# Squared norms of keys and queries added by matmul, accumulators of the first expert layer given back, other ranks in the plan

## The chip, the cores and the metric

The kernel runs on one core of a Trainium2 chip. The metric is device time in microseconds (us). A time is one execution; the kernel before ran three times and its median is the time before. The profile is of one further execution.

## The reference

Three layers in a row, all in float32 (weights come as 64-bit floats):

```python
def phi(x):                                  # x: [4, 8, 576, 64], omega: [128, 64]
    proj = np.einsum('bhsd,md->bhsm', x, omega)
    sq = np.sum(x * x, axis=-1, keepdims=True) / 2.0
    h = proj - sq
    h = h - np.max(h, axis=-1, keepdims=True)
    return np.exp(h) / np.sqrt(m)
q_p, k_p = (phi(q_s), phi(k_s))              # q, k scaled by 64 ** -0.25
kv = np.einsum('bhsm,bhsd->bhmd', k_p, v)
z = np.sum(k_p, axis=2)
num = np.einsum('bhsm,bhmd->bhsd', q_p, kv)
den = np.einsum('bhsm,bhm->bhs', q_p, z)[..., None] + 1e-06
x = (num / den)                              # as [2304, 512]
# first expert layer, d_ff 1536
g = x @ w_gate
x = g * (1.0 / (1.0 + np.exp(-g))) * (x @ w_val) @ w_out
# second, d_ff 2048: a piecewise quadratic of x @ w_in, then @ w_out
```

## The kernel before

**Attention.** Tokens lie on the 128 partitions for the values and on the free axis for keys and queries: one tile `ki`, `kl` or `qi` holds two layouts side by side, layout 0 with the 64 features of two heads on the partitions (`xb[:, 0]`) and layout 1 with tokens on the partitions (`xb[:, 1]`). `load` brings each with a DMA of its own. A group is one `k_group` (4 batches, 5 groups each of one or two units) or one `q_group` (9 blocks of 256 tokens, 2 halves `d`). `front` does the feature map of a group: `squares` turns layout 1 into squared norms, either with accumulating activations on ScalarE (L597) or with one square on ScalarE (L600) and one reduction on VectorE (L601); `proj` multiplies layout 0 by `omr` into two PSUM banks (L625; two 64-row halves of the array, one per head); VectorE takes the row maximum (L631) and adds the squared norm to it with two small reductions (L635); the exponential is taken by ScalarE straight from PSUM with that bias (L643), or by VectorE adding the bias (L647) and ScalarE taking the exponential in place (L651). Keys go on to the key-value sums (L690) and their copy (`kv_evac`), queries are transposed by a matmul (L763), copied into `qt`, and multiplied with the sums (`num`, L817); `norm` divides, and `x1_split` splits the block into a high and a low part in `x1s`.

**First expert layer.** `moe1` runs the early columns block by block as soon as `x1s` of a block is there: 24 matmuls of three-way split products per bank (`split3`, L400 to L402), then `elem1`, `row_out` into `hl`, and `out1`, which adds into two accumulator banks. These two banks are taken once, at the first block, and kept (`acc`); `acc_free` tells when `evac1` has read one. The rest of the first layer, and the second, run afterwards (`late_up`, `late_down`) with block products of a Strassen kind.

**What sets the order.** Nothing is scheduled by hand: `Planner` simulates the engines with given costs, takes the ready operation with the smallest rank on each engine, and emits instructions in that order, so every engine has one fixed queue. The ranks and start delays are the constants `PR_*` and `T_*`. All DMAs are issued from one queue (SP). There are 8 PSUM banks in one ring (`bank`); `bank_pair` takes two of them for a group of `front` or `num`.

Of the kernel before, what the change touches and what calls it, by code (L numbers as in the profile page):

```python
# [28 lines left out]
P = 128  # L29
# [17 lines left out]
NWL, NB1 = 7, 8  # L47
KINS, VINS, QINS, EBK, EBQ, N_QT = 3, 5, 2, 6, 4, 3
N_KL, N_QL, N_EL = 2, 1, 2

# [10 lines left out]

PR_K, PR_K0, PR_Q0, PR_Q = 1.04, 0.32, 0.17, 0.83
PR_C0, PR_C, PR_CS = 0.66, 0.90, 0.90
PR_W = 1.06
PR_BANK = 0.3
PR_ST, PR_X, PR_E = 1.50, 0.74, 1.45
T_V, T_Q0, T_C0 = 3.84, 2.87, 5.50
N_GATE, N_CS = 1, 3
N_WS = 2
# [205 lines left out]
def performer_moe_kernel(ctx: ExitStack, tc: tile.TileContext, qX, kX, vX, om, ident,  # L275
# [65 lines left out]
    omr = att.tile([P, P], F32, name="omr")  # L341
    ebufs = {False: ring(att, "ebk", EBK, [P, 512]), True: ring(att, "ebq", EBQ, [P, 512])}
    kin = ring(att, "ki", KINS, [P, 2, 512])
# [24 lines left out]
    lend(qin, "ql", N_QL, [P, 2, 512])  # L368
    lend(ebufs[False], "el", N_EL, [P, 512])
    nc.gpsimd.memset(rect.free[0][0][:, :, 32:33], 1e-6)  # L370
# [109 lines left out]
    def conv_feed():  # L480
        early = [(s, f) for p in range(NE) for s in ("g", "v", "o") for f in (2 * p, 2 * p + 1)]
        for i, kk in enumerate(early):
            if i == 0:
                yield T_C0
            if i == N_CS:
                yield q0_front
            yield from conv(kk, w_src(kk), wring, PR_C0 if i < 3 else late_rank)
        for kk in early[-2:]:
            yield wready[kk]
        for key in [kk for m, a, order, sets in passes for c in sets for kk in set_keys(m, c)]:  # L490
            t = yield Get(wtmp)
            pl.spawn(stage(key, t), PR_ST)
# [115 lines left out]

    def front(xb, n, loads, is_q, res, rng):

        st = yield Get(stat)
        sv = st.rearrange("p (a u) c -> p a u c", a=2)
        units = slice(0, 2 * n)
        sq_end = pl.spawn(squares(xb[:, 1], n, sv[:, :, :, 1], loads[1]), pl.cur.prio)
        es = []
        for a in range(2):
            es.append((yield Get(ebufs[is_q])))
        yield omr_ready
        yield loads[0]
        banks = yield from bank_pair()  # L620

        def proj():
            for u in range(2 * n):
                for a, h in enumerate(halves):
                    nc.tensor.matmul(banks[a][:, u * P:(u + 1) * P], xb[h, 0, u * P:(u + 1) * P], omr[h], start=True, stop=True,  # L625
                                     skip_group_check=True)
        yield Op("PE", 0.446 * n + 0.1, proj)
        pl.spawn(release(sq_end, rng, xb))
        pv = [ps[:, 0:256 * n].rearrange("p (u m) -> p u m", m=P) for ps in banks]
        for a in range(2):  # L630
            yield Op("DVE", c_dve(256 * n), lambda: nc.vector.tensor_reduce(  # L631
                out=sv[:, a, units, 0], in_=pv[a], axis=AX.X, op=ALU.max, negate=True))
        yield sq_end
        for i in range(2):
            yield Op("DVE", 0.12, lambda: nc.vector.tensor_reduce(  # L635
                out=sv[:, :, units, 2 + i], in_=sv[:, :, units, i:2 + i], axis=AX.X, op=ALU.add, negate=True))

        def expo(a):
            e, ps = es[a], banks[a]
            if pl.pick(ACT=2 * n * 0.262, DVE=c_dve(256 * n)) == "ACT":  # L640
# [14 lines left out]
        pl.put(stat, st)  # L655
        res.extend(es)

    kv_bank = {}

    def load(xb, src, n):  # L660
        src = src.rearrange("(p k c) -> p k c", p=P, k=2)
        return [pl.spawn(dma(xb[:, l, 0:256 * n], src[:, l], P * 1024 * n), pl.cur.prio) for l in range(2)]

    def k_group(b, gs, kb, prev):
        n = len(gs)
        es = []
        loads = load(kb, kX[b, gs[0] * 65536:(gs[0] + n) * 65536], n)
        yield from front(kb, n, loads, False, es, kin)
        for g in gs:
# [16 lines left out]
        def mm():  # L686
            for kp, v, u, pr, li in todo:
                for a in range(2):
                    for m, h in enumerate(halves):
                        nc.tensor.matmul(kp[h, 2 * pr + a, 0:65], es[a][:, u * P + 64 * m:u * P + 64 * m + 64],  # L690
                                         v[:, 65 * a:65 * a + 65], start=(li == 0 and a == 0),
                                         stop=(li == 8 or (li == 4 and pr == 0)), skip_group_check=True)
        yield Op("PE", 0.232 * len(todo) + 0.15, mm)
        for u in range(2 * n):
            i = 2 * gs[0] + u
            if i % 9 == 8:
                pl.spawn(kv_evac(b, i // 9), pl.cur.prio - 0.1)
        for e in es:
            back(ebufs[False], e)
        for g in gs:  # L700
# [32 lines left out]
    def k_stream():  # L733
        prev = Ev()
        pl.set(prev)
        for b in range(4):
# [4 lines left out]
            for gs in GROUPS:  # L741
                kb = yield Get(kin)
                prev = pl.spawn(k_group(b, gs, kb, prev), PR_K0 if b == 0 else PR_K)

    def q_group(k, d, qb):
        es = []
        yield from front(qb, 2, load(qb, qX[k, d], 2), True, es, qin)
        if k == 0:
# [7 lines left out]
        def turn(r):  # L756
            tp = yield Get(bank)

            def trans():
                for a in range(2):  # L760
                    for t in range(2):
                        u = 2 * r + t
                        nc.tensor.transpose(tp[:, (a * 2 + t) * P:(a * 2 + t + 1) * P], es[a][:, u * P:(u + 1) * P], ids)  # L763
            yield Op("PE", 4 * 0.11, trans)
            left[0] -= 1
            if left[0] == 0:
                for e in es:
                    back(ebufs[True], e)
            yield from copy(q_t[:, r].rearrange("p a t -> p (a t)"), tp, 512, False)
# [27 lines left out]
    def num(k, d, q_t):  # L797
# [11 lines left out]
        rc = yield Get(rec)  # L809
        banks = yield from bank_pair()  # L810

        def mm():
# [8 lines left out]
        yield from norm(*banks, rc, x)  # L821
        pl.put(rec, rc)
        yield from x1_split(k, d, x)
        yield from dma(half_block(x1d, k, d), x.rearrange("p (n t) -> p n t", n=2), P * 512 * 4)
# [107 lines left out]

    def evac1(k, d, last):
        rng = (osb, xin)[d] if k == NBLK - 1 else (xin, xpart)[d]
        if (k, d) in held:
            yield held_ready[k, d]
            x = held[k, d]
            yield Op("DVE", c_dve(512), lambda: nc.vector.scalar_tensor_tensor(
                out=x, in0=acc[d], scalar=0.5, in1=x, op0=ALU.mult, op1=ALU.add))
        else:  # L940
            if not last:
                held[k, d] = None
            x = yield Get(rng)
            yield from copy(x, acc[d], 512, False, 0.5)
        pl.set(acc_free[d])
        if not last:
# [63 lines left out]
    def out1(step, h_ev, res):  # L1010
# [7 lines left out]
        for n in range(KD):  # L1018
            d, c = divmod(n, 2)
            if first and c == 0:  # L1020
                yield acc_free[d]
                acc_free[d] = Ev()
            for i in range(2):
                yield Op("PE", 3 * c_pe(TB), lambda: split3(
                    acc[d][:, c * TB:(c + 1) * TB], ws[i][:, 0, n * P:(n + 1) * P], ws[i][:, 1, n * P:(n + 1) * P],
                    hl[:, 0, i * TB:(i + 1) * TB], hl[:, 1, i * TB:(i + 1) * TB],
                    first and c == 0 and i == 0, last and i == 1, True))
            if last and c == 1:
                pl.spawn(evac1(k, d, end))
        pl.put(hrow, res[1])  # L1030
# [4 lines left out]
    def moe1():  # L1035
        pend = None
        for step in steps1:
            k, fp = step
            if fp == 0:
                yield x1_ready[k]  # L1040
                if k == 0:
                    pl.set(moe_on)
                    for _ in range(2):
                        acc.append((yield Get(bank, -2)))
            xs = x1_tile[k]
# [601 lines left out]
```

## Time and profile before

| what | value |
|---|---|
| three runs | 955.35, 949.29, 953.86 us; median 953.86 us |
| the profiled execution, its own time | 949.58 us |
| its span, first to last instruction | 947.8 us |
| mean granted TensorE clock | 0.995 of full speed |
| PE (TensorE matmul) busy | 920.2 us, 97% |
| PEld (its weight loads) busy | 892.9 us, 94% |
| DVE (VectorE) busy | 799.7 us, 84% |
| ACT (ScalarE) busy | 515.2 us, 54% |
| POOL (GpSimd) busy | 67.6 us, 7% |

Busy shares are of the whole span. Matmuls are pipelined, so that a busy PE need not be a PE at its peak, and a stage is read by its own stretch of time. Of each matmul of attention with float32 operands by `omr` the trace has two records.

### The profile page before, as it was taken

Reading aid. Unit: us, or ns where it says so; the run is one execution under the profiler, and the core shown is the slowest. Engines: PE = TensorE matmul, PEld = TensorE weight load, DVE = VectorE, ACT = ScalarE, POOL = GpSimd, SP = SyncE. Lnnn points to the kernel's source line nnn. Section 1 sums busy time; section 2 is a strip of 40 time slices with the busy share of each in tenths; the row PEclk is TensorE's granted clock in tenths of the full one; section 3 lists DMA queues with packets and bytes.
Section 4 is the critical chain, followed back from the end, with each engine's and each line's share of the span. In section 5 each row is a group of like instructions: output and inputs, shape, how many; then the busy total and the mean of one; then the engine's idle time right before and its main releaser. Section 6 shows DMA issues by size and latency. Waiting matters only on the chain.

```text
span 947.8 us, 21783 instructions
## 1 busy us (share of the span) xinstructions
PE 920.2 (97%) x8708; PEld 892.9 (94%) x8708; DVE 799.7 (84%) x1536; ACT 515.2 (54%) x1226; POOL 67.6 (7%) x58
## 2 busy tenths in 40 slices
PE   7698989999999999999999999999999999999998
PEld 5588878999999999999999999999999999999998
DVE  7999998877989999999998999996698669866553
ACT  7988778653445454554454565554455445544331
POOL 0343332122100000000000000000000000000000
PEclk9899999999999999999999999999999999999999
DMA  8767596445848267665647654431323041403022
GB/s 284 272 204 238 176 292 217 168 168 184 260 166 278 64 228 226 222 209 177 190 170 232 209 181 155 137 127 63 123 68 112 6 141 46 133 13 100 1 90 90
DMA packets 91255, 152.12 MB, mean 160 GB/s; under 512 B 8592, under 2 KB 44432, under 8 KB 91152
## 3 DMA queue, kind: packets, MB, share of 16 engines
q1 hardware_dynamic: 91152, 150.72, 48.9%
q8 instruction: 68, 1.11, 0.5%
q14 instruction: 35, 0.29, 0.1%
HBM read 107.69 MB, written 42.99 MB: 159 GB/s over the span
## 4 chain that ended last, share of the span: by engine, by line
PE 64%; DVE 11%; DMA 6%; ACT 2%; issue 2%; SPq 0%; DVEq 0%; ACTq 0%
PE bank L400 20%; PE bank L401 20%; PE bank L402 20%; DMA ws<-in_w_dram 2%; DMA ws<-in_wo_dram 2%; PE bank L817 2%; DVE x1s L393 1%; PE bank L625 1%; DVE w L393 1%; DVE wt L424 1%; DVE wt L422 1%; DVE hb L1211 1%; PE bank L763 1%; DVE wb L393 1%; DVE xi L393 1%
## 5 line engine op out<-in xcount | busy, mean ns | idle before, releaser
L400 PE MATMUL bank<-x1s,w 128*128 128x256 f32 x492 | 138.7, 282 | 6.4 <-DVE hb L910 2.0
L402 PE MATMUL bank<-x1s,w 128*128 128x256 f32 x492 | 136.4, 277 | 0.0
L401 PE MATMUL bank<-x1s,w 128*128 128x256 f32 x492 | 136.3, 277 | 0.0
L400 PEld LDWEIGHTS bank<-x1s,w 128*128 128x128 f32 x492 | 92.4, 188 | 9.6 <-DVE hb L910 2.4
L402 PEld LDWEIGHTS bank<-x1s,w 128*128 128x128 f32 x492 | 92.6, 188 | 0.0
L401 PEld LDWEIGHTS bank<-x1s,w 128*128 128x128 f32 x492 | 92.4, 188 | 0.0
L400 PE MATMUL bank<-x1s,wb 128*128 128x256 f32 x286 | 79.1, 277 | 1.2 <-ACT eb L381 1.2
L402 PE MATMUL bank<-x1s,wb 128*128 128x256 f32 x286 | 79.0, 276 | 0.0
L401 PE MATMUL bank<-x1s,wb 128*128 128x256 f32 x286 | 79.0, 276 | 0.0
L400 PE MATMUL bank<-x1s,wx 128*128 128x256 f32 x278 | 77.4, 278 | 0.8 <-ACT eb L381 0.8
L381 ACT ACTIVATE x1s<-xq 128x512 fp32r<-128x512 f32 x80 | 50.2, 630 | 50.4 <-PE bank L402 20.7
L402 PE MATMUL bank<-x1s,wx 128*128 128x256 f32 x278 | 76.9, 277 | 0.6 <-POOL wx L391 0.6
L401 PE MATMUL bank<-x1s,wx 128*128 128x256 f32 x278 | 76.8, 276 | 0.0
L393 DVE TENSOR_TENSOR x1s<-xq,x1s 128x512 fp32r<-128x512 f32 x90 | 61.8, 686 | 9.6 <-ACT x1s L381 9.0
L417 ACT ACTIVATE wt<-ws 128x512 f32<-128x512 f32 x68 | 46.2, 682 | 41.7 <-DMA ws<-in_wo_dram 30.4
L381 ACT ACTIVATE eb<-bank 128x512 f32<-128x512 f32 x94 | 55.5, 591 | 22.3 <-PE bank L402 21.8
L400 PEld LDWEIGHTS bank<-x1s,wb 128*128 128x128 f32 x286 | 53.7, 188 | 1.4 <-ACT eb L381 1.4
L381 ACT ACTIVATE hlr<-hb 128x512 fp32r<-128x512 f32 x53 | 33.3, 631 | 38.8 <-PE bank L401 25.3
L402 PEld LDWEIGHTS bank<-x1s,wb 128*128 128x128 f32 x286 | 53.7, 188 | 0.0
L401 PEld LDWEIGHTS bank<-x1s,wb 128*128 128x128 f32 x286 | 53.7, 188 | 0.0
L400 PEld LDWEIGHTS bank<-x1s,wx 128*128 128x128 f32 x278 | 52.2, 188 | 1.4 <-ACT eb L381 1.2
L402 PEld LDWEIGHTS bank<-x1s,wx 128*128 128x128 f32 x278 | 52.2, 188 | 0.8 <-POOL wx L391 0.8
(247 smaller groups left out, 3347.8 us busy)
## 6 DMA issues: line engine op xcount, KB each, us to landing
ws<-in_w_dram SPq DMA_DIRECT2D x40, 512.0 KB, 4.9
ws<-in_wo_dram SPq DMA_DIRECT2D x28, 512.0 KB, 4.5
qi<-in_qX_dram SPq DMA_DIRECT2D x36, 256.0 KB, 4.7
xq<-x1d SPq DMA_DIRECT2D x36, 256.0 KB, 4.3
xq<-x2d SPq DMA_DIRECT2D x36, 256.0 KB, 3.9
ki<-in_kX_dram SPq DMA_DIRECT2D x28, 256.0 KB, 5.3
x1d<-os SPq DMA_DIRECT2D x18, 256.0 KB, 3.7
op<-os SPq DMA_DIRECT2D x18, 256.0 KB, 2.1
```

The source lines that it names most:

```text
L381: yield Op("ACT", c_act(n), lambda: nc.scalar.activation(dst, src, AF.Copy, scale=1.0 if scale is None else scale))
L393: yield Op("DVE", c_dve(n), lambda: nc.vector.tensor_tensor(out=dst, in0=a, in1=b, op=op), True)
L400: nc.tensor.matmul(ps, l_hi, r_hi, start=first, stop=False, skip_group_check=shared)
L401: nc.tensor.matmul(ps, l_hi, r_lo, start=False, stop=False, skip_group_check=shared)
L402: nc.tensor.matmul(ps, l_lo, r_hi, start=False, stop=last, skip_group_check=shared)
L417: yield Op("ACT", 0.575, lambda: nc.scalar.activation(t, hw.bitcast(F32), AF.Abs))
L422: yield Op("DVE", c_dve(512), lambda: nc.vector.scalar_tensor_tensor(out=ti, in0=lw, scalar=29, in1=ti, op0=ALU.logical_shift_right, op1=A ...
L424: yield Op("DVE", c_dve(512), lambda: nc.vector.scalar_tensor_tensor(out=ti, in0=hw, scalar=0xC0000000, in1=ti, op0=ALU.bitwise_and, op1=A ...
L625: nc.tensor.matmul(banks[a][:, u * P:(u + 1) * P], xb[h, 0, u * P:(u + 1) * P], omr[h], start=True, stop=True, skip_group_check=True)
L763: nc.tensor.transpose(tp[:, (a * 2 + t) * P:(a * 2 + t + 1) * P], es[a][:, u * P:(u + 1) * P], ids)
L817: nc.tensor.matmul(banks[what][h, r * TB + c0:r * TB + c1], kvr[b, d][:, r, a, halves[what]], q_t[:, r, a, c0:c1], start=True, stop=True, ...
L1211: yield Op("DVE", c_dve(n), lambda: nc.vector.scalar_tensor_tensor(out=h, in0=h, scalar=1.0, in1=g, op0=ALU.add, op1=ALU.mult), lock)
```

## The change

Three things. **Norms by TensorE:** for the keys of batches 0 and 1 and the queries of blocks 0 to 3, only layout 0 is loaded. Its square, times 1/16, is made into the other half of the same tile (`square_t`, on ScalarE or VectorE), and a second run of `proj` with a tile of -1 (`neg`) adds minus the squared norm onto the projection in PSUM. The row maximum then is the bias itself, and the two small reductions go. **Accumulators given back:** `out1` gets a bank when it begins a sum, and `evac1` returns it. **Ranks:** in `front` and `num` all that reads a bank pair ranks at most `PR_FRONT` = 0.35; `PR_K` is one number per batch, and other constants change. The exponential buffers of a group's two heads are now one tile.

```diff
-KINS, VINS, QINS, EBK, EBQ, N_QT = 3, 5, 2, 6, 4, 3
-N_KL, N_QL, N_EL = 2, 1, 2
+KINS, VINS, QINS, EBK, EBQ, N_QT = 3, 5, 2, 3, 2, 3
+N_KL, N_QL, N_EL = 2, 1, 1
-PR_K, PR_K0, PR_Q0, PR_Q = 1.04, 0.32, 0.17, 0.83
-PR_C0, PR_C, PR_CS = 0.66, 0.90, 0.90
+PR_K, PR_Q0, PR_Q = (0.32, 0.77, 0.91, 1.17), 0.17, 0.68
+PR_C0, PR_C, PR_CS = 0.66, 1.02, 1.13
+PR_FRONT = 0.35
-T_V, T_Q0, T_C0 = 3.84, 2.87, 5.50
-N_GATE, N_CS = 1, 3
+T_V, T_Q0, T_C0 = 3.0, 3.5, 7.0
+N_GATE, N_CS = 1, 6
+    neg = att.tile([P, P], F32, name="neg")
+    nc.gpsimd.memset(neg, -1.0)
+    def square_t(x, x2, m):
+        if pl.pick(ACT=c_act(m), DVE=c_dve(m)) == "ACT":
+            yield Op("ACT", c_act(m), lambda: nc.scalar.activation(x2, x, AF.Square, scale=0.25))
+        else:
+            yield Op("DVE", c_dve(m), lambda: nc.vector.scalar_tensor_tensor(
+                out=x2, in0=x, scalar=0.0625, in1=x, op0=ALU.mult, op1=ALU.mult), True)
...
-        sq_end = pl.spawn(squares(xb[:, 1], n, sv[:, :, :, 1], loads[1]), pl.cur.prio)
+        by_pe = len(loads) == 1
+        if not by_pe:
+            sq_end = pl.spawn(squares(xb[:, 1], n, sv[:, :, :, 1], loads[1]), pl.cur.prio)
         yield omr_ready
         yield loads[0]
+        if by_pe:
+            sq_end = pl.spawn(square_t(xb[:, 0, 0:256 * n], xb[:, 1, 0:256 * n], 256 * n), pl.cur.prio)
         banks = yield from bank_pair()
+        rank = pl.cur.rank
+        pl.cur.rank = min(pl.cur.prio, PR_FRONT)
...
-        yield Op("PE", 0.446 * n + 0.1, proj)
+        yield Op("PE", 0.446 * n + 0.1, lambda: proj(0, omr, True, not by_pe))
+        if by_pe:
+            yield sq_end
+            yield Op("PE", 0.446 * n + 0.1, lambda: proj(1, neg, False, True))
...
-                out=sv[:, a, units, 0], in_=pv[a], axis=AX.X, op=ALU.max, negate=True))
-        yield sq_end
-        for i in range(2):
-            yield Op("DVE", 0.12, lambda: nc.vector.tensor_reduce(
-                out=sv[:, :, units, 2 + i], in_=sv[:, :, units, i:2 + i], axis=AX.X, op=ALU.add, negate=True))
+                out=sv[:, a, units, 3 if by_pe else 0], in_=pv[a], axis=AX.X, op=ALU.max, negate=True))
+        if not by_pe:
+            yield sq_end
+            for i in range(2):
+                yield Op("DVE", 0.12, lambda: nc.vector.tensor_reduce(
+                    out=sv[:, :, units, 2 + i], in_=sv[:, :, units, i:2 + i], axis=AX.X, op=ALU.add, negate=True))
...
-        loads = load(kb, kX[b, gs[0] * 65536:(gs[0] + n) * 65536], n)
-        yield from front(kb, n, loads, False, es, kin)
+        loads = load(kb, kX[b, gs[0] * 65536:(gs[0] + n) * 65536], n, b > 1)
+        es = yield from front(kb, n, loads, False, kin)
...
-        yield from front(qb, 2, load(qb, qX[k, d], 2), True, es, qin)
+        es = yield from front(qb, 2, load(qb, qX[k, d], 2, k > 3), True, qin)
...
         banks = yield from bank_pair()
+        pl.cur.rank = min(pl.cur.prio, PR_FRONT)
...
             if first and c == 0:
-                yield acc_free[d]
-                acc_free[d] = Ev()
+                acc1[d] = yield Get(bank, -2)
...
-            yield from copy(x, acc[d], 512, False, 0.5)
-        pl.set(acc_free[d])
+            yield from copy(x, ps, 512, False, 0.5)
+        pl.put(bank, ps)
...
                 if k == 0:
                     pl.set(moe_on)
-                    for _ in range(2):
-                        acc.append((yield Get(bank, -2)))
```

Where the new order differs, at the two places that the prediction speaks of. The first is TensorE's queue just ahead of the first matmul of the first expert layer (that is the row with `x1s`). `omr` rows are projections, `vi` rows key-value sums, `qt` rows the numerators, `ids` rows transposes. Before:

```order
L625 MATMUL bank_70<-omr,qi_158 128x128
L625 MATMUL bank_69<-omr,qi_158 128x128
L817 MATMUL bank_66<-qt_142,kvr_0_160 64x256 x2
L817 MATMUL bank_65<-qt_142,kvr_0_160 64x256 x2
L690 MATMUL bank_64<-vi_136,ebk_145 64x65 x2
L690 MATMUL bank_64<-vi_136,ebk_146 64x65 x2
L400 MATMUL bank_70<-x1s_72,w_110 128x256
```

With the change (L639 is the projection's line, `neg` rows the added matmuls, L403 the old L400):

```order
L779 MATMUL bank_63<-ids,ebq_151 128x128 x4
L639 MATMUL bank_66<-omr,ki_154 128x128
L639 MATMUL bank_67<-omr,qi_155 128x128
L639 MATMUL bank_66<-neg,ki_154 128x128
L639 MATMUL bank_68<-omr,qi_156 128x128
L639 MATMUL bank_67<-neg,qi_155 128x128
L639 MATMUL bank_68<-neg,qi_156 128x128
L708 MATMUL bank_64<-vi_136,ebk_147 64x65 x12
L403 MATMUL bank_66<-x1s_72,w_110 128x256
```

The `x1s` row moved back: ahead of it stand now 208 projections and norm matmuls (104 with `omr`, 104 with `neg`) where there were 96, the same 108 key-value matmuls and 32 transposes, and 16 numerators in place of 32. Between a projection and its `neg` matmuls mostly another group's matmuls stand. In all the queue has 8042 matmuls instead of 7906, the 136 more being the `neg` ones.

The second place is ScalarE's queue ahead of the activation that writes the last piece of the first `x1s` block. `ebk`, `ebq` rows are exponentials, L597 accumulating squares, L600 whole squares, L417 a step of a weight's conversion. Before:

```order
L600 ACTIVATE qi_159<-qi_159 128x512
L600 ACTIVATE ki_157<-ki_157 128x512
L417 ACTIVATE wt_79<-ws_77 128x512
L643 ACTIVATE ebk_149<-bank_66,st_129 128x128 x2
L597 ACTIVATE ki_156,st_126<-ki_156 128x64 x8
L381 ACTIVATE qt_142<-bank_66 128x512
L793 ACTIVATE os_103<-bank_64 128x512
L381 ACTIVATE x1s_72<-os_103 128x512
```

With the change (L614 the square of layout 0, L661 the exponential from PSUM, L669 that in place, L384 a copy):

```order
L614 ACTIVATE ki_154<-ki_154 128x512
L384 ACTIVATE kvr_1_158<-bank_69 128x4x64
L808 ACTIVATE os_102<-bank_65 128x512
L661 ACTIVATE ebq_150<-bank_70,st_130 128x128 x4
L661 ACTIVATE ebk_149<-bank_67,st_129 128x128 x2
L661 ACTIVATE ebq_151<-bank_66,st_122 128x128 x4
L384 ACTIVATE qt_142<-bank_67 128x512
L384 ACTIVATE x1s_72<-os_103 128x512
```

What stands ahead of that row over the whole queue: before 48 L597, 9 L600, 26 L643 and 12 L651; now no accumulating square, 12 L614, 56 L661 and 6 L669; and five smaller instructions fewer. From TensorE's instruction 1757 of before on (1893 of the change) its queue is the same, 6149 matmuls long.

## Rows read from the trace of the kernel before

**Rows 1.** Page, busy time of each engine over the span

```profile
PE 920.2 (97%) x8708; PEld 892.9 (94%) x8708; DVE 799.7 (84%) x1536; ACT 515.2 (54%) x1226; POOL 67.6 (7%) x58
```

**Rows 2.** Windows: length, busy us (records) of PE, PEld, DVE, ACT, POOL; clock, DMA, GB/s

```profile
5.16:12.75 7.59, 3.41 (x41) 3.03 (x40) 5.63 (x16) 4.26 (x23) 0.00 (x0) 1.00 0.98 346
12.75:30.00 17.25, 17.25 (x294) 15.15 (x296) 17.15 (x40) 17.04 (x68) 0.11 (x1) 0.90 0.95 315
30.00:53.00 23.00, 15.72 (x176) 11.72 (x172) 22.03 (x55) 21.90 (x86) 10.63 (x8) 0.85 0.73 245
53.00:184.00 131.00, 124.92 (x1534) 112.44 (x1535) 120.34 (x262) 102.55 (x372) 40.35 (x32) 1.00 0.68 218
184.00:260.00 76.00, 76.00 (x706) 72.17 (x705) 60.88 (x116) 32.62 (x63) 16.12 (x12) 1.00 0.61 200
700.00:750.00 50.00, 50.00 (x443) 50.00 (x443) 42.76 (x77) 25.06 (x45) 0.00 (x0) 1.00 0.19 63
```

**Rows 3.** Waits of PE, 5 to 53 us: who waited for whom, total, times, longest

```profile
PE bank L625 <- DMA qi<-in_qX_dram: 3.6, 1, 3.6
PE bank L625 <- ACT ebq L643: 2.9, 1, 2.9
PE bank L625 <- ACT kvr L381: 2.0, 1, 2.0
PE bank L763 <- ACT qt L381: 1.4, 1, 1.4
```

**Rows 4.** Timeline of PE: start, us, instructions merged

```profile
53.04 0.38 PE L400 MATMUL bank<-x1s,w 128*128 128x256 f32 x1
59.67 0.39 PE L400 MATMUL bank<-x1s,w 128*128 128x256 f32 x1 [0.35 <-DVE qt L383]
...
61.24 1.16 PE L625 MATMUL bank<-omr,ki 64*128 64x128 f32 x16
62.33 0.38 PE L400 MATMUL bank<-x1s,w 128*128 128x256 f32 x1
...
67.35 1.03 PE L763 MATMUL bank<-ids,ebq 128*128 128x128 f32 x8
68.14 0.36 PE L400 MATMUL bank<-x1s,w 128*128 128x256 f32 x1
...
74.94 1.39 PE L690 MATMUL bank<-vi,ebk 128*64 128x65 f32 x40
76.25 1.16 PE L625 MATMUL bank<-omr,qi 64*128 64x128 f32 x16
...
214.56 3.67 PE L817 MATMUL bank<-qt,kvr 128*64 128x256 f32 x32
218.17 1.09 PE L763 MATMUL bank<-ids,ebq 128*128 128x128 f32 x8
```

**Rows 5.** Groups by form, 0 to 230 us: busy, mean ns, idle before

```profile
L635 DVE TENSOR_REDUCE st<-st 128x8 f32<-128x16 f32 x68 | 10.6, 162 | 0.5
L647 DVE TENSOR_TENSOR ebk<-bank,st 128x512 f32<-128x512 f32 x16 | 10.7, 684 | 0.1
```

**Rows 6.** Timeline of ACT: start, us, instructions merged

```profile
25.58 0.24 ACT L597 ACTIVATE qi<-qi 128x64 f32<-128x64 f32 x1
25.82 0.24 ACT L597 ACTIVATE qi<-qi 128x64 f32<-128x64 f32 x1
...
36.25 3.19 ACT L643 ACTIVATE ebq<-bank,st 128x128 f32<-128x128 f32 x12
39.26 0.71 ACT L651 ACTIVATE ebq<-ebq 128x512 f32<-128x512 f32 x1
39.78 0.71 ACT L600 ACTIVATE qi<-qi 128x512 f32<-128x512 f32 x1
...
47.80 0.74 ACT L381 ACTIVATE x1s<-os 128x512 fp32r<-128x512 f32 x1
```

**Rows 7.** Waits of PE, 53 to 184 us, the longest of nine

```profile
PE bank L400 <- ACT qt L381: 1.7, 1, 1.7
```

## What the change is expected to do

> **What bounds the kernel now.** I read the busy line first, then the windows by stage, then the waits of TensorE, and last its timeline for the price of each kind of matmul. TensorE is busy 97% of the span [rows 1], and from 184 to 260 us it never idles: 76.00 of 76.00 us, with VectorE at 80% [rows 2]. From its instruction 1757 on its queue is word for word the same in both kernels. So the end moves by what happens before that point, one for one: by matmul time added, less TensorE time that was lost there and no longer is. No later work can give anything back or take anything away, unless another engine falls behind.
>
> Lost time before 184 us lies in two stretches. In the head, from the first projection at 5.16 us to the first matmul on `x1s` at 53.04 us, ScalarE and VectorE bound: from 12.75 to 53 us they are busy 38.9 and 39.2 of 40.25 us, while TensorE idles 7.3 us between 30 and 53 us and its granted clock is 0.90 and 0.85, a mix of the 2.4 and 1.2 GHz levels [rows 2]. It idles 4.2 us before 12.75 us too, when the DMA share is 0.98 [rows 2]; its longest wait in the head, 3.6 us, is for a query load, the next three, 6.3 us in sum, are for ScalarE [rows 3]. In the middle, 53 to 184 us, TensorE is busy 124.9 of 131 us and VectorE 120.3 [rows 2]: the two are nearly level.
>
> **Prices.** Eight projections in a run take 62.33 - 61.24 = 1.09 us, 0.136 each; eight transposes 0.79, 0.099 each; twenty key-value matmuls 76.25 - 74.94 = 1.31, 0.066 each; sixteen wide numerators 218.17 - 214.56 = 3.61, 0.226 each [rows 4]. A matmul of the expert layers costs 50 / 443 = 0.113 [rows 2]. Twelve of them between attention runs take 61.24 - 59.67 = 1.57 us instead of 1.36 [rows 4], so each such interruption costs 0.21.
>
> **What is added.** The 136 norm matmuls have the shape and type of projections: 136 x 0.136 = 18.5 us, all on TensorE and all before 184 us. If each run cost its record's 1.16 us [rows 4], it would be 17 x 1.16 = 19.7; I take 18.5, since runs follow each other at that pace.
>
> **What the head gives back.** The order puts 96 projections, 108 key-value matmuls, 32 transposes and 32 wide numerators ahead of the first `x1s` matmul: 13.1 + 7.1 + 3.2 + 7.2 = 30.6 us of work in 47.9 us, 17.3 us lost. With the change it is 208 projections and norms, 108, 32 and 16 numerators: 28.3 + 7.1 + 3.2 + 3.6 = 42.2 us. How much of it is waited for? ScalarE's queue up to the last piece of `x1s`: 48 accumulating squares at 0.24 go (11.5), 30 exponentials from PSUM at 3.01 / 12 = 0.25 come (7.5), six exponentials in place at 0.52 go (3.1), 3 squares come, two of them half width (about 1.1), five smaller ones go (about 2) [rows 6]. That is 8 us less, where its end before was at 48 us [rows 6], so `x1s` could be there at about 40 us; 42.2 us of TensorE work from 5.16 us on ends at 47.4 us at best. TensorE becomes the head's bound. VectorE loses over the whole attention 36 small reductions at 0.16, and of full-width passes at 0.68 nine reductions of squares and nine bias additions, and gets two squares: 16.7 us less by durations [rows 5]. 18 loads, 4.5 MB, go from SP's queue, 13 us at 346 GB/s [rows 2]; the queries come no later for it, and their wait is filled with 20 norm matmuls of keys (2.7 us), 4.2 us becoming 1.5. For the rest I take 2.5 us, 7% of the 36 us left, a little more than the 3% that ScalarE and VectorE lost when they were the bound. Head loss 4.0, so **13.3 us come back** and the first `x1s` matmul starts at 51.4 us. Bounds: 2.6 (the 3% instead) and 11.8 (the three ScalarE waits of 6.3 us stay, and 4 us for load and half clock).
>
> **What the middle gives back.** Before: 131 - 124.9 = 6.1 us idle, and 39 interruptions of expert-layer work x 0.21 = 8.2; 14.3 lost. The new order has 25 interruptions, 5.3 us. Of the idle time I keep 2.7, since VectorE has less to do per matmul there. Loss 8.0, **6.3 come back**; bounds 14 (nothing, if new waits fill the room) and 5.3.
>
> How much room that stretch has can be judged in two ways. Its busy TensorE leaves 6.1 us, its weight loads 131 - 112.4 = 18.6 [rows 2]. The Trainium skill (Perfetto Trace Analysis, Identifying the Most-Contended Engine) says that matmul busy time is a poor measure of TensorE's headroom and the weight loads' busy share a good one. By the first my middle can hardly gain more than it does, by the second it could gain twice that; I take the first and keep the second as a rival.
>
> **At nothing.** The returned accumulators: none of TensorE's nine waits in the middle, the longest 1.7 us [rows 7], is for the copy of an accumulator, so nothing of the two freed banks is counted beyond the idle time taken off above; if that cover fails, these short waits are what comes back. The merged exponential buffers hold as much as before. The fill of `neg` on POOL comes ahead of its first work.
>
> **Sum.** 18.5 - 13.3 - 6.3 = -1.1 us. The profiled execution took 949.58 us (span 947.8), 4.3 below the median of the runs, 953.86; I put the difference on the median: **952.8 us**, no change that shows. About 1% of this kernel, 9.5 us, is what a measurement can tell.
>
> **Rivals.** *Slower: TensorE waits for the square.* Each norm run stands in TensorE's fixed queue and needs a square from ScalarE, queued there among exponentials; whatever stands behind it on TensorE waits too, and through it ScalarE's next exponentials. Its price is one full-width ScalarE step with its handover, 0.71 us by its record [rows 6], up to 2.9 where ScalarE is late [rows 3]. With 17 runs x 0.71 = 12.1 us, of which 2 us are in the sum's losses already, it gives 953 + 10 = 963 us. It decides (slower by 1%) from some 0.7 us a run. Against it: in the order other groups' matmuls stand between most projections and their norms. For it: ScalarE stays the producer of all that TensorE waits for in the head, and a bank pair is held longer. The Trainium skill (TensorEngine Tiling, PSUM Bottleneck) says that packing small matmuls speeds TensorE but not the emptying of PSUM, which speaks against gaining from matmuls here; the three waits for ScalarE agree with it.
>
> *Faster: all lost time but the unavoidable goes.* Head loss 2.6, middle 5.3 and no idle: 18.5 - 14.7 - 9.0 = -5.2; should the 25 interruptions cost half as much too, -7.8: 946 us. For it: the weight loads' share above, and TensorE denser in the head, so that its granted clock may stay at 2.4 GHz. Against it: VectorE still at some nine tenths in the middle.
>
> *The relief is not used.* ScalarE and VectorE are freed, but the head stays bound by order, with the first `x1s` matmul at 56 us (head loss 8.6), and the middle gains its fewer interruptions alone, 2.9: 18.5 - 8.7 - 2.9 = +6.9, 961 us.
>
> **Chances.** Forecast 0.55, its own range 948 to 958. Faster rival 0.20. Relief not used 0.12. Slower rival 0.13. The range reaches from 944 to 963 us. Faster by over 1%, below 944.3: 0.14, the far part of the faster rival and the spread of the runs. Slower by over 1%, above 963.4: 0.13, the slower rival in full, or relief not used and more. Within: 0.73.
>
> **What would show it.** Right: the first `x1s` matmul between 50 and 54 us, with a clock near full in 12 to 53 us; ScalarE and VectorE clearly under 97% there; 25 interruptions, and some 3 us of idle TensorE from there to the steady part; the same rows later, shifted by about -1 us. Wrong: waits of the `neg` rows for ScalarE of 0.5 us and more, run after run (slower), or `x1s` before 49 us (faster). The forecast falls if a norm run costs other than 1.09 us, or if TensorE idles more after 184 us than it did.

## The result and the profile after

The changed kernel takes 941.49 us (median of five runs, 939.58 to 943.20), the kernel before beside it 949.62 (949.29 to 955.35). The ratio is 0.9894, 95% interval 0.9860 to 0.9928; below, each ratio has its interval behind it. The forecast, 952.8 us and "no change that shows", is missed by 11 us, and the time lies below the range's lower end of 944. The profiled execution after took 939.58 us (span 937.8), 10.0 less than that of before.

The busy line of the page after, to be set beside [rows 1]:

```profile
PE 927.0 (99%) x8980; PEld 902.7 (96%) x8980; DVE 787.0 (84%) x1483; ACT 509.2 (54%) x1126; POOL 65.1 (7%) x57
```

The windows after, columns as in [rows 2]:

```profile
5.16:12.75 7.59, 6.47 (x120) 6.21 (x120) 4.44 (x8) 3.81 (x11) 0.00 (x0) 1.00 0.98 327
12.75:30.00 17.25, 17.25 (x312) 15.39 (x312) 13.96 (x27) 16.64 (x43) 2.51 (x2) 1.00 0.64 214
30.00:53.00 23.00, 22.22 (x319) 18.99 (x318) 22.79 (x44) 19.89 (x68) 5.86 (x4) 1.00 0.61 183
53.00:184.00 131.00, 130.74 (x1650) 119.36 (x1650) 115.37 (x247) 102.92 (x338) 41.62 (x33) 1.00 0.64 208
```

TensorE idles 2.2 us from 5.16 to 184 us where it idled 17.5; its granted clock is 1.00 in the head, and the DMA share from 12.75 to 30 us is 0.64 instead of 0.95. All of TensorE's waits after, 5.16 to 184 us, to be set beside [rows 3, 7]:

```profile
PE bank L639 <- DMA qi<-in_qX_dram: 1.1, 1, 1.1
PE bank L779 <- DVE rect L796: 1.0, 2, 0.8
```

No norm run waits for its square. TensorE's timeline after, to be set beside [rows 4]:

```profile
12.35 1.06 PE L639 MATMUL bank<-neg,qi 64*128 64x128 f32 x16
13.24 1.06 PE L639 MATMUL bank<-omr,qi 64*128 64x128 f32 x16
14.13 1.06 PE L639 MATMUL bank<-omr,kl 64*128 64x128 f32 x16
15.03 1.06 PE L639 MATMUL bank<-neg,qi 64*128 64x128 f32 x16
16.02 1.39 PE L708 MATMUL bank<-vi,ebk 128*64 128x65 f32 x40
17.33 1.16 PE L639 MATMUL bank<-neg,kl 64*128 64x128 f32 x16
18.43 1.09 PE L779 MATMUL bank<-ids,ebq 128*128 128x128 f32 x8
...
47.41 0.38 PE L403 MATMUL bank<-x1s,w 128*128 128x256 f32 x1
...
228.09 3.67 PE L833 MATMUL bank<-qt,kvr 128*64 128x256 f32 x32
```

The same matmul of the kernel before:

```profile
236.15 3.67 PE L817 MATMUL bank<-qt,kvr 128*64 128x256 f32 x32
```

A norm run of eight matmuls, from its start to that of what follows, takes 0.89 us between other projection runs (the row at 12.35 us), 0.99 with another kind on one side (15.03) and 1.10 with other kinds on both (17.33). The first `x1s` matmul starts at 47.41 us, 5.63 earlier than before; forecast 51.4. The last numerator matmul, where the attention ends on TensorE, starts at 228.09 instead of 236.15 us: 8.06 less. The other 1.9 of the profiles' 10.0 us come later, where TensorE's waits are shorter (3.5 us from 184 us on, 4.8 before).

### The profile page after: what moved, and what is told of

Same layout as the page of the kernel before. It is cut to its first block, busy times and chain, and to the rows that moved or that the text cites. A ratio compares the mean times of both kernels' runs of the same rounds, so it can differ in the third digit from the quotient of the medians.

```text
span 937.8 us, 22182 instructions
## 1 busy us (share of the span) xinstructions
PE 927.0 (99%) x8980; PEld 902.7 (96%) x8980; DVE 787.0 (84%) x1483; ACT 509.2 (54%) x1126; POOL 65.1 (7%) x57
## 4 chain that ended last, share of the span: by engine, by line
PE 76%; DVE 15%; DMA 4%; issue 2%; ACT 2%; SPq 1%; DVEq 0%; ACTq 0%
PE bank L403 23%; PE bank L404 22%; PE bank L405 22%; PE bank L639 3%; PE bank L833 3%; PE bank L779 1%; PE bank L708 1%; DMA xq<-x2d 1%; DMA ws<-in_w_dram 1%; DVE st L648 1%; DVE x1s L396 1%; DVE wt L427 1%; DVE wt L425 1%; DMA ws<-in_wo_dram 1%; DVE xq L396 1%
## 5 line engine op out<-in xcount | busy, mean ns | idle before, releaser
L403 PE MATMUL bank<-x1s,w 128*128 128x256 f32 x492 | 137.4, 279 | 0.4 <-DVE eb L1235 0.4
L403 PEld LDWEIGHTS bank<-x1s,w 128*128 128x128 f32 x492 | 92.4, 188 | 1.6 <-DVE eb L1235 0.6
L403 PE MATMUL bank<-x1s,wb 128*128 128x256 f32 x286 | 79.2, 277 | 1.7 <-ACT eb L384 1.0
L384 ACT ACTIVATE x1s<-xq 128x512 fp32r<-128x512 f32 x80 | 50.2, 629 | 54.1 <-PE bank L405 23.2
L403 PE MATMUL bank<-x1s,wx 128*128 128x256 f32 x278 | 77.2, 278 | 1.0 <-ACT eb L384 1.0
L384 ACT ACTIVATE eb<-bank 128x512 f32<-128x512 f32 x94 | 55.6, 591 | 23.6 <-PE bank L405 23.2
L648 DVE TENSOR_REDUCE st<-bank 128x4 f32<-128x512 f32 (+1 forms) x76 | 47.9, 655 | 11.2 <-PE bank L639 11.2
L403 PEld LDWEIGHTS bank<-x1s,wb 128*128 128x128 f32 x286 | 53.7, 188 | 2.1 <-ACT eb L384 1.2
L384 ACT ACTIVATE hlr<-hb 128x512 fp32r<-128x512 f32 x53 | 33.4, 632 | 41.0 <-PE bank L404 26.2
L403 PEld LDWEIGHTS bank<-x1s,wx 128*128 128x128 f32 x278 | 52.2, 188 | 1.4 <-ACT eb L384 1.2
```

What stands on the lines that cost most here:

```text
L384: yield Op("ACT", c_act(n), lambda: nc.scalar.activation(dst, src, AF.Copy, scale=1.0 if scale is None else scale))
L403: nc.tensor.matmul(ps, l_hi, r_hi, start=first, stop=False, skip_group_check=shared)
```

## The experiments

Theories at first: **N**, the norms' relief made the gain; **R**, the ranks; **A**, the two banks given back. All kernels were timed in five rounds beside the kernel before, whose medians lay between 949.6 and 951.2 us; ratios are to it.

### One part undone at a time

```diff
 no_norms:  loads of both layouts, no neg matmul (b > 1, k > 3 become True)
 no_ranks:  old PR_*, T_* and N_CS values; the three PR_FRONT lines out
 no_acc:
-                acc1[d] = yield Get(bank, -2)
+                yield acc_free[d]; acc_free[d] = Ev()     # banks taken at the first block, kept
 merge_only: all three undone; the merged exponential buffers stay
```

> The changed kernel without the norms by TensorE: all keys and queries load both layouts and take the old way through squares and small reductions; returned accumulators, ranks and merged buffers stay. Theory N (the gain of 8 us comes from the work that the norms take off ScalarE, VectorE and the DMA queue in the head): 948 to 956 us, first expert-layer matmul at 52 us or later, granted clock of 0.85 to 0.95 between 12 and 53 us. Theory R (the gain comes from the new ranks, the norms only add 16 us of TensorE work): at or under 941 us.

> The changed kernel with the two accumulator banks of the early columns kept as before. Theory A (the two banks are what took the idle time out of the middle): 945 us or more, with 3 us or more of TensorE waits between 53 and 184 us that name copies out of banks. Theories N and R: 939 to 944 us, under 1 us of such waits.

> The changed kernel with the old ranks and start delays, and without the common rank of what reads a bank pair; norms by TensorE and returned accumulators stay. Theory R: 947 us or more. Theory N: 939 to 944 us, first expert-layer matmul still at 47 to 49 us.

> The kernel before with nothing but the merged exponential buffers (one tile for a group's two heads, as many columns). All theories: 948 to 952 us, no difference. If it moves by 3 us or more, a new plan by itself is worth as much as the parts that are told apart here.

Measured: no_norms 944.92 (0.9943, 0.9923 to 0.9964), no_ranks 945.62 (0.9946, 0.9925 to 0.9967), no_acc 958.69 (1.0087, 1.0065 to 1.0110), merge_only 967.29 (1.0182, 1.0158 to 1.0205). Undoing norms or ranks costs 3 to 4 us, which meets neither N's nor R's ranges; undoing the accumulators costs 17, as A said. merge_only, expected at no difference, is 17 us slower than the kernel before. TensorE's longest waits with both accumulators kept (no_acc), 5.16 to 184 us:

```profile
PE bank L403 <- DVE ebq L665: 7.2, 3, 3.6
PE bank L403 <- ACT ebk L661: 2.3, 1, 2.3
...
PE bank L403 <- DVE ebk L665: 1.2, 1, 1.2
```

L403 multiplies `x1s` by weights; neither `ebq` nor `ebk` is its operand. What those instructions share with it is a bank: they read the one that L403 will write. So these are waits for a free bank: 9.1 us from 53 to 184 us with the smaller ones, 0.3 in the changed kernel. One more of them, ahead of 53 us, in TensorE's timeline of no_acc (start, us, instructions merged, idle before):

```profile
46.67 1.39 PE L708 MATMUL bank<-vi,ebk 128*64 128x65 f32 x40
50.77 0.39 PE L403 MATMUL bank<-x1s,w 128*128 128x256 f32 x1 [2.71 <-DVE ebq L665]
```

and VectorE's timeline of the same kernel, the last piece of `x1s`:

```profile
44.51 0.68 DVE L396 TENSOR_TENSOR x1s<-os,x1s 128x512 fp32r<-128x512 f32 x1
```

The block was there at 45.2 us. TensorE was done with what stands ahead at 48.06; the block's first matmul then waited 2.71 us for a bank, since the accumulators are taken just ahead of it. In the changed kernel as many matmuls stand ahead of that row, and it starts at 47.41.

### Only the accumulators; one of two

```diff
 acc_base: the kernel before, and
-                yield acc_free[d]
-                acc_free[d] = Ev()
+                acc1[d] = yield Get(bank, -2)
...
-        pl.set(acc_free[d])
+        pl.put(bank, ps)
 one_acc: the changed kernel, accumulator d = 0 kept, d = 1 given back
```

> The kernel before, with one edit: the two accumulators of the first mixture are taken when a run of steps starts and given back when they are copied out. Theory A (free banks set the pace of the attention stage; the two banks are free about half of the time): faster by 8 to 17 us, 933 to 942, TensorE's waits for readers of exponential banks gone, first x1s matmul at 48 to 53 us. Rival S (scatter of the order: any edit gives a new written order and the times of orders lie 10 us apart for no single reason): anywhere from 940 to 965, and no special shift of the waits for bank readers. Theory N (the norms made the gain): within 3 us of before, 947 to 953.

> The changed kernel, with one of its two accumulators kept for good (as before), the other given back. Theory A: between the changed kernel (941.5) and the one that keeps both (958.7), 946 to 954. Rival S: no such order, anywhere from 938 to 962; at 941 or less, or 959 or more, A's dose is refuted.

Measured: acc_base 947.88 (0.9968, 0.9949 to 0.9988), a gain of 3 us where A said 8 to 17; one_acc 944.06 (0.9919, 0.9892 to 0.9946), 2.6 above the changed kernel, below A's 946. The banks are not worth a fixed number of us each. That brought up rival **S**: each edit makes another written order, and orders have luck.

### How much luck an order has

One cost of the planner's table, that of a projection or norm run, is moved by 0.002 us; nothing else changes but the order.

```diff
-        yield Op("PE", 0.446 * n + 0.1, lambda: proj(0, omr, True, not by_pe))
+        yield Op("PE", 0.446 * n + 0.102, lambda: proj(0, omr, True, not by_pe))   # or 0.098, both runs
```

> The changed kernel with one cost in the planner's table 0.002 us higher (the projection run), which alone gives another written order; nothing else is changed. Theory A and N (the parts make the gain, whatever the order): 940 to 943. Rival S (orders scatter by several us): 944 to 950, with waits before 184 us that the changed kernel does not have.

> The changed kernel with both accumulators kept (958.7 us), and one cost in the planner's table 0.002 us lower (the projection run), which alone gives another written order. Theory A (the two banks are worth 17 us): 955 to 962. Rival S (much of the 17 us is the luck of that one written order): 942 to 952.

> The changed kernel with the cost of a projection run in the planner's table 0.002 us lower, which alone gives another written order; the pair to the same order's table with both accumulators kept (948.4 us). Theory A, as the runs left it (the accumulators are worth some us, the order scatters by as many): 940 to 945, 4 to 8 us under its pair. Rival S (the accumulators are worth nothing, the difference is the luck of orders): within 3 us of its pair, 945.5 to 951.

> The changed kernel with both accumulators kept and the same cost 0.002 us higher; the pair to the changed kernel with that cost (945.5 us). Theory A, as the runs left it: 950 to 956, 4 to 10 us over its pair. Rival S: within 3 us of its pair, 942.5 to 948.5.

| table cost | given back | both kept | difference |
|---|---|---|---|
| 0.100 | 941.49 (0.9894) | 958.69 (1.0087) | 17.2 |
| 0.102 | 945.49 (0.9941, 0.9923 to 0.9960) | 959.20 (1.0089, 1.0070 to 1.0109) | 13.7 |
| 0.098 | 940.54 (0.9894, 0.9875 to 0.9914) | 948.38 (0.9977, 0.9962 to 0.9991) | 7.8 |

Both hold in part. Three orders of each kind scatter by 5 us with the banks given back and by 11 with them kept, so the 3 to 4 us of no_norms and no_ranks, and the 17 of merge_only, are not settled by one order each. The accumulators stand clear of it, as far as three pairs tell: in each the kernel that returns them wins, by 7.8 to 17.2 us, and the slowest order with the banks returned (945.49) is faster than the fastest that keeps them (948.38). The second pair's 959.20 lies even above the 950 to 956 expected. The third pair has another symptom. TensorE's longest waits in nudge_no_acc, 5.16 to 184 us:

```profile
PE bank L639 <- DMA qi<-in_qX_dram: 1.9, 1, 1.9
PE bank L403 <- DVE ebk L665: 0.7, 1, 0.7
```

Hardly a wait for a bank, but in its written order attention matmuls interrupt the expert layer 41 times before the last numerator, against 21 in its pair, 24 and 25 in the other two orders that give the banks back, and 30 and 34 in the other two that keep them. At the forecast's 0.21 us each, 20 more make 4.2 of the 7.8 us, an estimate. My reading, not shown further: a plan with six banks either waits for one or weaves around it.

### Fixed orders: the norm matmuls, the relief, the loads

These change no row of the written order but the ones they leave out or add, so S has no part in them. In the changed order:

```diff
 skip_norm:   neg run left out:   yield Op("PE", 0.446 * n + 0.1, None)
 norm_twice:  neg run issued twice
 load_both:   in load, by_pe groups:
+        also = ((xb[:, 1, 0:256 * n], src[:, 1]),)     # second DMA right behind the first
```

> The changed kernel with the 136 norm matmuls left out (the exponentials lack the norm term), everything else in the same written order on every engine. Theory P (TensorE is the bound, the norm matmuls cost their full price of 0.11 to 0.136 us each): 15 to 18.5 us less, 923 to 927. Rival O (ScalarE and VectorE still set the pace of the head, the norm matmuls fill gaps): 0 to 6 us less, 935 to 941, TensorE idle by 10 us and more before 53 us.

> The changed kernel in its own written order with each norm run issued twice (136 matmuls more; the norm is subtracted twice). Leaving the 136 out had moved the time by less than 1 us. Theory B (TensorE and its suppliers are level in this order: the 136 just fill the gaps): the second 136 find none and cost 12 to 16 us, 953 to 958. Rival O (the suppliers alone set the pace): 0 to 6 us, 941 to 948.

> The changed kernel in its own written order, with the second copies of the 18 groups of keys and queries loaded again as before (4.5 MB more, each behind the first copy; the square overwrites them). Theory D (the head is set by loads, and the gain came from loading less): 5 to 10 us more, 946 to 951, TensorE waiting for loads and its granted clock below full in the head. Rival W (the written order makes the gain, the loads fit beside it): within 2 us of the changed kernel, 940 to 943.5.

Measured: skip_norm 941.03 (0.9885, 0.9856 to 0.9914), norm_twice 954.30 (1.0035, 1.0019 to 1.0051), load_both 949.16 (0.9975, 0.9957 to 0.9994). The 136 norm matmuls cost 0.5 us, that is nothing, against P; 136 more cost 12.8, against O and as B said: TensorE and its suppliers are level there. Windows of skip_norm:

```profile
5.16:12.75 7.59, 4.95 (x73) 4.45 (x72) 4.86 (x9) 3.97 (x11) 0.00 (x0) 1.00 0.98 319
12.75:30.00 17.25, 16.31 (x260) 14.29 (x262) 13.71 (x28) 17.22 (x46) 2.51 (x2) 0.90 0.66 223
30.00:53.00 23.00, 17.86 (x218) 13.37 (x216) 22.90 (x45) 19.47 (x67) 5.86 (x4) 1.00 0.56 180
53.00:100.00 47.00, 44.65 (x594) 39.46 (x589) 44.98 (x99) 44.01 (x162) 15.88 (x12) 0.96 0.72 236
53.00:184.00 131.00, 127.74 (x1571) 116.16 (x1565) 114.63 (x244) 103.10 (x337) 41.69 (x33) 0.99 0.63 208
```

Without the norm matmuls TensorE idles 12.0 us from 5.16 to 184 us instead of 2.2, and its granted clock falls to 0.90 and later 0.96, while ScalarE (17.22 of 17.25), then VectorE (22.90 of 23) are as full as with them. That is rival O's picture, with 8.7 us of idle TensorE before 53 us where O said 10. With norm_twice TensorE is the bound:

```profile
53.00:100.00 47.00, 47.00 (x674) 41.88 (x673) 39.60 (x84) 38.58 (x131) 10.65 (x8) 1.00 0.64 202
100.00:150.00 50.00, 50.00 (x719) 44.51 (x720) 44.80 (x101) 42.72 (x151) 11.38 (x9) 1.00 0.60 195
53.00:184.00 131.00, 131.00 (x1739) 118.16 (x1738) 113.89 (x244) 101.07 (x331) 40.21 (x32) 1.00 0.62 198
```

load_both takes 7.7 us more, as theory D (the loads) said. Its head:

```profile
12.75:30.00 17.25, 15.47 (x224) 14.52 (x226) 11.39 (x22) 13.02 (x35) 0.00 (x0) 0.80 0.78 258
30.00:53.00 23.00, 20.66 (x324) 17.52 (x321) 17.83 (x36) 18.65 (x53) 8.77 (x6) 1.00 0.81 273
```

ScalarE and VectorE have room, TensorE idles and its clock is 0.80; the first `x1s` matmul starts at 56.41 us. Part of this may be the wait and not the transfer: the square overwrites the second copy and so has to wait for it. ScalarE's waits for key and query loads, 5.16 to 53 us, are 10.3 us here, 4.0 in the changed kernel:

```profile
ACT qi L614 <- DMA qi<-in_qX_dram: 5.6, 2, 4.7
ACT ki L614 <- DMA ki<-in_kX_dram: 4.7, 2, 2.6
```

In the order of before, the norms' three effects one by one. The change touches 18 groups; two of them are half as wide, so their projections are as many as 17 full runs, 136 matmuls. Doubled projections stand here for the norm matmuls; they don't wait for a square.

```diff
 proj_twice:     the projections of the 18 groups issued twice
 relief:         of their squares one ScalarE pass stays, sums and reductions go
 relief_twice:   relief, and projections twice
 relief_noload:  relief, and no load of their second layout (the square reads the first)
 relief_noload_twice: that, and projections twice
```

> The kernel before with the projections of the same 17 groups issued twice in the same run (136 matmuls more into the same bank, no other work, the same order on every engine). Theory P2 (the lost time of the head cannot take in matmuls that stand on the producers' path): 14 to 18.5 us more, 964 to 969. Rival O2 (the head has idle TensorE time, and a clock that rises with more activity): 3 to 10 us more, 953 to 960, with first x1s matmul within 3 us of its 53.0 before.

> The kernel before in its own written order, with the relief of the 17 groups alone: of their squares one plain full-width ScalarE square stays, the accumulating squares, the VectorE reductions of squares and the small sums are left out (56 and 10 and 36 instructions; the exponentials of these groups lack the norm term). No norm matmul. By rows of before this takes some 10 us of ScalarE and 13 us of VectorE. Theory O (ScalarE and VectorE set the pace up to about 100 us, TensorE does not): 7 to 12 us less, 939 to 944, first x1s matmul before 49 us. Rival P (TensorE is the bound outside the head's 17 us): 2 to 5 us less, 946 to 949.

> The same, and the projections of the 17 groups issued twice (136 matmuls more at the place where they stand). Theory O: within 4 us of the run with the relief alone, since the matmuls fill gaps that are there anyway. Rival P: 8 to 18 us more than the relief alone, at or above the kernel before (951).

> The kernel before in its own written order, with the relief of ScalarE and VectorE for the 17 groups and without the loads of their second copies (the square reads the first copy; the exponentials of these groups lack the norm term). No norm matmul. Theory D: 6 to 10 us less than before, 940 to 945, where the relief alone gave 1.7. Rival W: within 2 us of the relief alone, 947 to 950.

> The same, and the projections of the 17 groups issued twice (136 matmuls). Theory D: the matmuls fill gaps left by loads, so with the loads gone they cost more than the 7 to 8.5 us they cost in this order before: 10 to 15 us over the run without them. Rival W: again 7 to 9 us over it, 954 to 958 in all.

| in the order of before | us | ratio, interval |
|---|---|---|
| proj_twice | 959.61 | 1.0087, 1.0056 to 1.0118 |
| relief | 948.94 | 0.9985, 0.9972 to 0.9998 |
| relief_twice | 956.18 | 1.0063, 1.0039 to 1.0088 |
| relief_noload | 941.91 | 0.9899, 0.9876 to 0.9922 |
| relief_noload_twice | 950.47 | 0.9989, 0.9972 to 1.0007 |

Relief alone is worth 1.4 us (0.15% of 951), with the loads gone 9.6: the loads make the difference, 7.0 to 8.2 (7.0 by the two medians), as D said and against O; relief's 948.94 lies in the range of rival P. The matmuls cost 8.3 in the order of before (O2, though the first `x1s` matmul moves by 3.4 us, not 3), 7.2 with the relief, 8.6 with the loads gone too (D's 10 to 15 is missed); all three together come to -1.0, and the interval takes in no difference at all. In the old order, then, the norms by TensorE are worth nothing that shows. The window that relief left behind:

```profile
12.75:30.00 17.25, 17.13 (x296) 15.06 (x294) 14.61 (x28) 13.46 (x29) 1.01 (x1) 0.91 0.94 324
```

and that of relief_noload:

```profile
12.75:30.00 17.25, 14.44 (x250) 12.08 (x244) 16.51 (x32) 14.55 (x33) 3.85 (x3) 1.00 0.77 235
```

Relieved, ScalarE and VectorE only idle (13.46 and 14.61 of 17.25) behind a DMA share of 0.94; without the loads the share is 0.77, and VectorE is nearly full again (16.51), with later work. The first `x1s` matmul moves from 52.24 to 47.08 us.

## Why the prediction was wrong

**The step that failed: "At nothing. The returned accumulators".** The forecast put the two banks at nothing; in the changed kernel they are worth 7.8 to 17.2 us, in three pairs of orders. I looked for a wait named after an accumulator's copy [rows 7] and, finding none, took the banks to be free of charge. But all eight banks are one ring, and a matmul that lacks one waits for whoever reads the bank it is given, under that reader's name. Read so, most of the waits already shown are waits for a bank: a projection does not use `ebq` or `kvr`, a transpose of `ebq` does not use `qt` [rows 3], and L400 does not use `qt` [rows 7]; 8.0 us in sum. Such a wait is still one for the reader, which is late with that bank. More rows of TensorE's waits before, 5.16 to 184 us:

```profile
PE bank L400 <- DVE hb L910: 1.4, 1, 1.4
...
PE bank L763 <- ACT ebk L643: 1.0, 2, 0.7
...
PE bank L400 <- DVE ebq L647: 0.5, 1, 0.5
```

With these and five smaller ones (1.7) it is 8.0 + 2.9 + 1.7 = 12.6 us of bank waits before, 1.0 after (the `rect` row). Not all of them are the accumulators' doing. The two banks are taken just ahead of the first `x1s` matmul, so 7.3 of the 12.6 us, before 53 us, fell while all eight banks served the attention; all of these name ScalarE. The old kernel with the banks returned, acc_base, still waits 10.9 us for banks: 7.4 before 53 us, and 3.5 instead of 5.3 later. Its longest:

```profile
PE bank L625 <- ACT ebq L643: 3.3, 1, 3.3
...
PE bank L400 <- DVE ebk L647: 2.3, 1, 2.3
PE bank L625 <- ACT kvr L381: 2.0, 1, 2.0
```

The 7.3 us left the changed head without them: no_acc, which keeps the accumulators, has 1.0 us of bank waits there ahead of its first `x1s` matmul. It was rather the norms' part, as far as one order each tells: no_norms has 3.9 us of them and more before 53 us, no_ranks none that the view lists. What the two banks are worth is shown by the pairs and not by this list. The Trainium skill (Perfetto Trace Analysis, Optimization Strategy) says that a gap which keeps coming back on the engine that should be full can mean too little PSUM for the next tile; the pairs agree, 7.8 to 17.2 us. In the three orders that keep the accumulators but have all else, the times are 958.69, 959.20 and 948.38: the forecast of 952.8 lies among them, as does its first `x1s` matmul at 51.4 (50.77, 50.53, 52.97). So the sum came out near the change without its second part, in part by luck: these orders lie 11 us apart, in two of them that row waits 2.71 us for a bank, which the forecast did not have, and other terms of the sum were wrong, as follows. On the old kernel alone the banks bring only 3 us; why the changed kernel needs them more (its bank pairs wait for a square and a second run, and its producers load less) is argued, not shown.

**What bounds the kernel now** came out half right. In the head I read ScalarE and VectorE at 38.9 and 39.2 of 40.25 us as the bound, and the DMA share only before 12.75 us, though the next window showed 0.95 [rows 2]. The relief that I costed in detail brings 1.4 us by itself; the loads, which I let pass with "the queries come no later for it", bring 7.0 to 8.2 more once the relief is there, and 7.7 in the changed order. What the loads bring without the relief no run shows.

**What is added, 18.5 us.** The price of a run, 1.09 us, came from a projection run that stands alone between other kinds [rows 4]. Many norm runs stand beside other projections and take 0.89 or 0.99; summed along the timeline, all 136 matmuls take some 16.5 us, an estimate. More important, it was taken as a cost: in the changed order it is 0.5 us. Without these matmuls the suppliers need as long; the first `x1s` matmul starts 1.4 us earlier (46.03), the last numerator not at all (228.89). TensorE, given less to do, idles 9.8 us more before 184 us and loses some 3.6 us to the lower clock (an estimate: 0.10 of 17.25 us and 0.04 of 47). In the old order doubled projections cost 7 to 9, still half.

**What the head gives back**: 17.3 at the prices of the forecast (42.2 us of work in 42.25 us), against 13.3 and beyond the bound drawn (a loss of 2.6 at least). The end I called "47.4 at best" is where it ended. **What the middle gives back**: 25 interruptions as read from the order; the stretch from the first `x1s` matmul to the last numerator went from 183.11 to 180.68 us, -2.43 where the forecast's terms make +0.6, so 9.3 back instead of 6.3, just beyond the bound drawn (a loss of 5.3, 9.0 back). Of the two measures of room, busy time was nearly used up: from 53 to 184 us it rose by 5.8 of 6.1 us, to 130.74 of 131. The Trainium skill (Perfetto Trace Analysis, Identifying the Most-Contended Engine) judges TensorE's headroom by the weight loads' busy share; they rose from 112.4 to 119.4 us. No run shows that the 11.6 us left there can be used: with norm_twice TensorE is busy 131.00 us, its weight loads 118.16, and the matmuls added cost 12.8 us.

**The base.** The -1.1 was put on the median of three runs, 953.86; the median of five is 949.62. That is 4 of the 11 us missed. By ratio the miss is the difference between -0.1% and -1.1%.

**Rivals.** "TensorE waits for the square" did not come: no `neg` row is among the waits. The faster rival was nearest (-5.2 to -7.8 against -8.1), and its sign, `x1s` before 49 us, was seen; but its reasons named lost time on TensorE and not the banks or the loads. The sign is weak besides: nudge_after2 is as fast with its first `x1s` matmul at 57.54 us, since its order puts 72 matmuls more ahead of it.

Open: what merged buffers, ranks and norms are worth each, apart from the luck of an order; that would need many orders of each. No cost was moved in the kernel before either, so how lucky its own order is, and how much of the 8 us is owed to that, is not known.

## What to carry to other kernels

Ask of every wait whether the named producer makes an operand; if it does not, the wait is for a buffer, here a PSUM bank, and whatever holds one for long can have a price though no wait bears its name. Such a list of waits does not give the price; runs with the buffer held and given back, in several orders, do. Matmuls put on an engine whose suppliers need longer are free until it is level with them (0.5 us for 136 here) and cost most of their time beyond that (12.8 us for 136 more); leave them out, and double them, in a fixed order to find the level. Where a planner writes the order, move one of its costs by a hair and time that first: an effect smaller than this scatter can't be read from one edit.

## What the runs showed of the hardware

Less work on TensorE lowered its granted clock. In the changed order, 12.75 to 30 us, it is 1.00 with the norm matmuls and 0.90 without; when loads delayed them, 0.80, each a mix of the 2.4 and 1.2 GHz levels. In the order of before, doubled projections raised it from 0.90 and 0.85 [rows 2] to 1.00 and 0.93 (proj_twice):

```profile
12.75:30.00 17.25, 17.25 (x322) 15.66 (x322) 16.04 (x37) 15.17 (x59) 0.00 (x0) 1.00 0.87 299
30.00:53.00 23.00, 17.87 (x238) 15.04 (x240) 20.07 (x49) 20.83 (x85) 9.61 (x7) 0.93 0.70 220
```

A part of what the added matmuls cost there may have come back as clock: 0.10 of 17.25 us and 0.08 of 23 are 3.6 us, an estimate.
